# Six places instead of four for the raw sequence blocks of a DFT and MLP kernel's y phases

## The chip, the cores and the metric

The kernel runs on one core of a Trainium2 chip. Its metric is the time of one execution on the device, in microseconds (us). Matmuls run on TensorE, elementwise work on VectorE and ScalarE, a few small operations on GpSimd, and every DMA is issued from SyncE's queue (SP), in the order of the program.

## The reference

A sequence of 2048 rows with 512 features goes through four residual layers, a Fourier mixing layer and an MLP in turn, twice. Everything is float32.

```python
def _A_ref(x, dft_seq_re, dft_seq_im, dft_hid_re, dft_hid_im):
    a = jnp.einsum("bsd,ed->bse", x, dft_hid_re)
    b = jnp.einsum("bsd,ed->bse", x, dft_hid_im)
    return jnp.einsum("ts,bse->bte", dft_seq_re, a) - jnp.einsum("ts,bse->bte", dft_seq_im, b)

def _B_ref(x, w1, w2, w3, w4):
    h = _gelu(_layernorm(x) @ w1)
    hs = (four groups of columns, shifted by +1, -1, +2, -2 rows) @ w2
    x1 = x + hs
    return x1 + _gelu(_layernorm(x1) @ w3) @ w4

x = x + _A_ref(_layernorm(x), ...)
x = x + _B_ref(_layernorm(x), ...)
x = x + _A_ref(_layernorm(x), ...)
x = x + _B_ref(_layernorm(x), ...)
```

## The kernel before, in words

**Stages.** There are two layers, 0 and 1, each a Fourier mixing layer and an MLP. The mixing layer works on four chunks `c` of 512 output columns of the sequence. A chunk has an *x phase* and then a *y phase*, except that chunk 0 of layer 0 has one plain phase. Each phase has eight steps `k`, one for each pair of 128-row tiles of the sequence. The products with the hidden matrices (`hs`) of chunk `c - 1` are woven into the x phase of chunk `c`; after chunk 3 they stand alone, and the MLP (`by_pairs`) follows.

**Products in three matmuls.** Every float32 operand is split into a high part (a cast on ScalarE) and a low part (a subtraction on VectorE), and a product is three matmuls of 128x128 by 128x512: high by high, high by low, low by high (`mm3`, lines 282 to 284). A step of an x or y phase calls `mm_half`, which makes six matmuls. A y step `k` calls it four times, so 24 matmuls.

**Raw blocks and the ring.** The sequence weights (`ws`) come from DRAM in *pieces* of 128x1024 floats, 512 KB, into one of four *places* `raw0` to `raw3`. From a place, the engines make an *item* in one of four *ring* slots: `stage_one` makes the sum and the high part, `stage_two` the low part. A y step takes one pair of pieces and makes two items of it, `by1` and `by0`. Each is a difference of the two pieces (VectorE, L234), its high part (ScalarE, L235) and its low part (VectorE, L245). An x step makes a plain item (cast on ScalarE, L228, low part on VectorE, L245) and an item `one` (L230, L231, L245) of one piece. `stream()` hands the next item to the matmuls, after `prefetch` has made as many later ones as the ring has room for.

**What sets the order.** The code runs in the order in which it is written (a manual schedule), so each engine's list of instructions is fixed when the kernel is built. A semaphore lets an instruction wait for the writer or the last reader of its data. `issue_dma` emits loads of pieces as early as the rule allows: piece `i` goes to place `i % 4`, and its DMA is emitted once the stages that read piece `i - 4` have been emitted. On SP's queue it then waits for these readers, and everything behind it waits as well. Other DMAs stand in the same queue: `X1` loads and stores (`tmp` to and from `x1d`), reloads of tiles `xs` from `x1d` in chunk 3, and the turned tile (`turned0` stored to `zd`, L604, and read back into `zt0f`, L609), which the MLP's first products need.

**Memory.** All these tiles lie in one arena at fixed word addresses. `EXT` is a region of six tiles of 512 words, of which the tile `ay4` takes four during the mixing layer. `STG` is a region of 1024 words that holds staged MLP weights: `w4_raw` is loaded there at hook 2 of some x phases and read at hook 10. The places `raw0` to `raw3` lie at `RAWS` and share their memory with the MLP's scratch tiles `rest0` to `rest7` and `gt`.

Of the kernel before, what the change touches and what calls it, by code (L numbers as in the profile page):

```python
# [8 lines left out]
F32 = mybir.dt.float32  # L9
# [5 lines left out]
S, D, F = 2048, 512, 1376  # L15
# [4 lines left out]
CH = 512  # L20
# [14 lines left out]
RAW = 4  # L35
# [8 lines left out]
def spectral_mlp_kernel(ctx: ExitStack, tc: tile.TileContext, x, ws, hs, w1, w2, w34, out):  # L44
# [35 lines left out]
    EXT = RNG + RING * 4 * CH  # L80
    RAWS = EXT + 6 * D
    STG = RAWS + RAW * 2 * CH + 32
    nc.alloc_sbuf_tensor("arena", [P, STG + 2 * CH], F32)

    def at(name, word, *shape, dtype=F32R):
        return nc.alloc_sbuf_tensor_at(name, [P, *shape], dtype, offset=base + 4 * word).ap()

    def both(name, word, *shape):
        return at(name, word, *shape), at(name + "f", word, *shape, dtype=F32)
# [13 lines left out]
    rg = [[at(f"rg{i}{g}", RR + (4 * i + g) * 2 * CH, 2, CH) for g in range(KD)] for i in range(2)]  # L103
    ring, ringf = zip(*(both(f"ring{i}", RNG + i * 4 * CH, 2, 2, CH) for i in range(RING)))
    raw_at = [at(f"raw{i}", RAWS + i * 2 * CH, 2, CH, dtype=F32) for i in range(RAW)]

    blk, blkf = {}, {}
    for i, word in (("11", H3), ("21", H3 + 4 * CH), ("12", RNG), ("22", RNG + 4 * CH)):
# [15 lines left out]
    def xt(j):  # L124
        return xs[j // 2][:, j % 2]
# [17 lines left out]
        return tmps[(count["tmp"] - 1) % len(tmps)]  # L143


    pieces, items, w_items, w_pieces = [], [], [], []

    def piece(src, a=0, b=2):
        pieces.append((src, a, b))
        return len(pieces) - 1  # L150

    def item(kind, *ids, span=(0, 2), dest=None):
        items.append((kind, ids, span, dest))

    def y_order():
        order = [(k, kind) for k in range(NP) for kind in ("by1", "by0")]
        order[-3], order[-2] = order[-2], order[-3]
        return order

    for layer in range(LAYERS):  # L160
        for c in range(NC):
            if layer == 0 and c == 0:
                for k in range(NP):
                    item("plain", piece(ws[c, k][:, 2:4]))
                    item("plain", piece(ws[c, k][:, 0:2]))
                continue
            for k in range(NP):
                if c:
                    for h in range(NP):
                        if HAT[h] == k:  # L170
                            item("plain", piece(hs[HORDER[h % 4]]))
                p = piece(ws[c, k][:, 2:4])
                item("plain", p)
                item("one", p, span=(0, 1))
            ps = [(piece(ws[c, k][:, 2:4]), piece(ws[c, k][:, 0:2])) for k in range(NP)]
            for k, kind in y_order():
                item(kind, *ps[k])
        for o in HORDER:
            item("plain", piece(hs[o]))
        w_items.append(len(items))  # L180
        for i in range(2):
            item("plain", piece(w1[i]), dest=w12[i])
        for i in range(2):
            item("plain", piece(w2[i]), dest=w12[2 + i])
        w_pieces.append(len(pieces))
    uses = {}
# [1 line left out]
        for i in it[1]:  # L188
            uses.setdefault(i, []).append((n, "two" if it[0] == "plain" else "one"))
    raws, slots, sums = {}, {}, {}  # L190
    state = {"dma": 0, "one": 0, "two": 0, "use": 0, "made": 0, "done": 0, "limit": 0, "load": w_pieces[0]}
    x_left = [(0, 1), (1, 1)] + [(j, 2) for j in range(2, NT, 2)]

    def load_x():
        if x_left:
            j, n = x_left.pop(0)
            rows(xs[j // 2][:, j % 2 : j % 2 + n], x, j, n, True)
# [5 lines left out]
    def issue_dma(upto=None):  # L203
        while state["dma"] < (state["load"] if upto is None else upto):
            i = state["dma"]
            if i >= RAW and any(n >= state[stage] for n, stage in uses[i - RAW]):
                break
            src, a, b = pieces[i]
            raws[i] = raw_at[i % RAW]
            nc.sync.dma_start(raws[i][:, a:b], src)  # L210
            state["dma"] += 1
            if i % 2 and i > 3:
                load_x()
# [154 lines left out]
    def xp_sums(k):  # L368
        ax_sums(k)
        ay_sums(k)  # L370
# [1036 lines left out]
    def w4_split(i):  # L1407
        for n in (i - 5, i - 4, i - 3):
            if 0 <= n <= NF:
                w, wf = w4_in[n % 4]  # L1410
                if n == i - 5:
                    nc.vector.tensor_tensor(w[:, 1], wf[:, 1], w[:, 0].bitcast(F32), op=ALU.subtract)
                    nc.sync.dma_start(w4_from[n][1], w.bitcast(F32))
                elif n == i - 4:
                    nc.scalar.copy(w[:, 0], wf[:, 1])
                else:
                    nc.sync.dma_start(wf[:, 1], w4_from[n][0])
# [26 lines left out]
    for layer in range(LAYERS):  # L1444
# [4 lines left out]
        for c in range(NC):  # L1449
            if layer == 0 and c == 0:  # L1450
                raws[0] = raw_at[0]
                for i in (1, 0):
                    load_x()
                    nc.sync.dma_start(raws[0][:, i], pieces[0][0][:, i])
# [84 lines left out]
            def hook(i):  # L1539
                k, odd = divmod(i, 2)  # L1540
                if layer == 0 and c == 1:
                    if i == 1:
                        xp_sums(NP - 1)
                    if i == 2:
                        xp_highs(NP - 1, False)
                    if i == 3:
                        xp_lows(NP - 1, False)
                    w4_split(2 * NP + i)
                if c == 0:
                    if layer:  # L1550
                        for step, f in zip((0, 0, 1), (ay_sums, ay_highs, ay_lows)):
                            if i == step:
                                f(5)
                            if i == step + 10:
                                f(6)
                        for k, first, stages in (
                            (6, X6, (xp_stats, xp_norm, ax_sums, ax_highs, ax_lows)),
                            (7, X7, (xp_stats, xp_norm, ax_sums, ax_highs, ax_lows)),
                        ):
                            for step, f in zip((0, 1, 3, 4, 6), stages):  # L1560
                                if i == first + step:
                                    f(k)
                    return
                if (layer, c) in W4_AT:
                    w4_sums(W4_AT[layer, c], i)
                j = (c - 1) * TC
                if i == 4:
                    rows(X1, xin, j, 2, True)
                if i == 9:
                    rows(X1, x1d, j, 2, False)  # L1570
                if i == 10:
                    rows(X1, xin, j + 2, 2, True)
                if c == NC - 1 and i in BACK:
                    rows(xs[BACK[i] // 2], x1d, BACK[i], 2, True)
                if c == NC - 1 and i in (12, 15):
                    for j in (0, 1) if i == 12 else (2, 3):
                        normed_act(tmp[:, j], xt(j), ln2[j])
# [16 lines left out]
                    turn_in(ztf[0])  # L1594

            y_phase(c, hook)

        tmps[:] = singles
        count["tmp"] = 0
# [79 lines left out]
```

## Time and profile before

| | |
|---|---|
| runs | 1429.75, 1428.42, 1429.76 us; median 1429.75 |
| the profiled execution's own time | 1429.24 us |
| its span, first to last instruction | 1427.3 us |
| TensorE busy | 1420.0 us, 6261 matmuls |
| VectorE busy | 1168.8 us |
| ScalarE busy | 732.1 us |
| granted TensorE clock | 1.00 |
| DMA | 307.57 MB, mean 215 GB/s |

The span leaves out 1.9 us at the ends of the execution, so a change of the span is a change of the time. In the rows of the profile, a timeline row has the start in us, the duration in us, the engine, the line, the operation and the tiles (out, then in); in brackets stands how long the engine was idle just before and which instruction ended that. A row of the chain has the start, the duration and what the chain went through. PE is TensorE, DVE VectorE, ACT ScalarE, and SPq is SyncE's DMA queue.

### The profile page before, as it was taken

How to read it: one execution, taken by the hardware profiler on the slowest of the kernel's cores; microseconds unless marked ns; L12 is line 12 of the kernel's file. 1: busy time of each engine (PE TensorE's matmuls, PEld its weight loads, DVE VectorE, ACT ScalarE, POOL GpSimd, SP SyncE). 2: the span in 40 equal slices, each digit the busy share in tenths (PEclk: the TensorE clock that was granted, in tenths of full speed). 3: DMA queues.
4: the chain of work that ended last, by engine and by line, in shares of the span. 5: the costliest groups of instructions: out<-in, count | busy, mean ns of one | idle time of the engine just before them, and what ended most of it. 6: DMA issues, size and time to landing. Idle time of an engine off the chain costs nothing.

```text
span 1427.3 us, 17317 instructions
## 1 busy us (share of the span) xinstructions
PE 1420.0 (99%) x6261; PEld 1173.8 (82%) x6261; DVE 1168.8 (82%) x1642; ACT 732.1 (51%) x992; POOL 79.7 (6%) x105
## 2 busy tenths in 40 slices
PE   9999999999999999999999999999999999999998
PEld 7888888888888888888888888888877888888887
DVE  7986998988979888666799989889889787656676
ACT  5663464455565754434455644544555665433351
POOL 2100000000002000000000000000000020000000
PEclk9999999999999999999999999999999999999999
DMA  7866656657754857944645566575777458477764
GB/s 253 278 207 206 206 191 223 212 175 270 270 163 121 290 199 253 362 159 164 223 160 191 182 231 211 175 244 184 232 250 240 139 156 309 159 243 282 241 206 159
DMA packets 127828, 307.57 MB, mean 215 GB/s; under 512 B 9216, under 2 KB 50176, under 8 KB 124544
## 3 DMA queue, kind: packets, MB, share of 16 engines
q1 hardware_dynamic: 127744, 306.48, 64.2%
q8 instruction: 49, 0.80, 0.2%
q14 instruction: 35, 0.29, 0.1%
HBM read 252.18 MB, written 54.26 MB: 215 GB/s over the span
## 4 chain that ended last, share of the span: by engine, by line
PE 96%; DVE 2%; DMA 2%; issue 0%; SPq 0%; ACT 0%; DVEq 0%
PE psd L283 10%; PE psd L282 10%; PE psd L284 10%; PE psa L283 8%; PE psa L282 8%; PE psa L284 8%; PE psc L283 7%; PE psc L284 7%; PE psc L282 7%; PE psb L283 7%; PE psb L282 7%; PE psb L284 7%; DMA raw<-in_ws 2%; DVE ring L245 1%; DVE ring2f L234 0%
## 5 line engine op out<-in xcount | busy, mean ns | idle before, releaser
L228 ACT CAST ring<-raw 128x1024 fp32r<-128x1024 f32 x127 | 132.9, 1052 | 80.3 <-PE psd L284 41.1
L245 DVE TENSOR_TENSOR ring<-raw,ring 128x1024 fp32r<-128x1024 f32 x126 | 153.4, 1219 | 12.8 <-ACT ring L228 12.6
L282 PE MATMUL psd<-ring,rr 128*128 128x512 f32 x208 | 80.9, 389 | 0.0
L283 PE MATMUL psd<-ring,rr 128*128 128x512 f32 x208 | 80.9, 389 | 0.0
L284 PE MATMUL psd<-ring,rr 128*128 128x512 f32 x208 | 80.9, 389 | 0.0
L322 POOL TENSOR_TENSOR rs<-ve,mhalf 128x4 f32<-128x4 f32 x16 | 28.7, 1796 | 609.6 <-DVE nm L321 609.6
L301 POOL TENSOR_TENSOR rs<-ve,mhalf 128x2 f32<-128x2 f32 (+2 forms) x33 | 28.8, 872 | 547.5 <-DVE nb L300 528.6
L235 ACT CAST ring<-ring0f 128x1024 fp32r<-128x1024 f32 x28 | 29.5, 1054 | 57.7 <-DVE ring0f L234 57.7
L619 ACT ACTIVATE tmp<-rest 128x512 f32<-128x512 f32 x30 | 19.0, 632 | 73.2 <-DVE rest L468 72.8
L245 DVE TENSOR_TENSOR ring<-ring1f,ring 128x512 fp32r<-128x512 f32 (+1 forms) x56 | 53.2, 950 | 0.7 <-ACT ring L231 0.7
L330 ACT ACTIVATE tmp<-xs,nb,rs 128x512 f32<-128x512 f32 x56 | 43.2, 808 | 14.4 <-POOL nb L302 13.1
L283 PE MATMUL psb<-ring,ay 128*128 128x512 f32 x128 | 50.2, 392 | 0.4 <-DVE ring L245 0.4
L283 PE MATMUL psc<-ring,ay 128*128 128x512 f32 x128 | 49.9, 390 | 0.3 <-DVE ring L245 0.3
L282 PE MATMUL psb<-ring,ay 128*128 128x512 f32 x128 | 49.8, 389 | 0.0
L284 PE MATMUL psb<-ring,ay 128*128 128x512 f32 x128 | 49.8, 389 | 0.0
L284 PE MATMUL psc<-ring,ay 128*128 128x512 f32 x128 | 49.8, 389 | 0.0
L282 PE MATMUL psc<-ring,ay 128*128 128x512 f32 x128 | 49.8, 389 | 0.0
L235 ACT CAST ring<-ring1f 128x1024 fp32r<-128x1024 f32 x28 | 29.5, 1054 | 39.2 <-DVE ring1f L234 39.2
L282 PE MATMUL psa<-ring,ay 128*128 128x512 f32 x126 | 49.2, 390 | 0.3 <-ACT rr00f L501 0.3
L283 PE MATMUL psa<-ring,ay 128*128 128x512 f32 x126 | 49.1, 389 | 0.0
L282 PE MATMUL psd<-ring,ay 128*128 128x512 f32 x126 | 49.0, 389 | 0.0
L283 PE MATMUL psd<-ring,ay 128*128 128x512 f32 x126 | 49.0, 389 | 0.0
(657 smaller groups left out, 4439.9 us busy)
## 6 DMA issues: line engine op xcount, KB each, us to landing
raw<-in_ws SPq DMA_DIRECT2D x183, 512.0 KB, 5.0
w4r<-w4d SPq DMA_DIRECT2D x66, 512.0 KB, 4.4
raw<-in_hs SPq DMA_DIRECT2D x56, 512.0 KB, 3.6
w3b<-w3d SPq DMA_DIRECT2D x14, 1792.0 KB, 7.9
w3d<-w3b SPq DMA_DIRECT2D x5, 1792.0 KB, 6.9
x1d<-tmp SPq DMA_DIRECT2D x12, 512.0 KB, 6.2
xs<-x1d SPq DMA_DIRECT2D x12, 512.0 KB, 5.2
w4d<-w4in SPq DMA_DIRECT2D x11, 512.0 KB, 5.0
```

Source lines behind the costliest of these rows:

```text
L228: nc.scalar.copy(dest[:, a:b, 0], r[0][:, a:b])
L235: nc.scalar.copy(dest[:, :, 0], lo)
L245: nc.vector.tensor_tensor(lo, src, hi.bitcast(F32), op=ALU.subtract)
L282: nc.tensor.matmul(o, lh, rh, start=first, stop=False, skip_group_check=more)
L283: nc.tensor.matmul(o, lh, rl, start=False, stop=False, skip_group_check=more)
L284: nc.tensor.matmul(o, ll, rh, start=False, stop=last, skip_group_check=more)
L301: nc.gpsimd.tensor_tensor(rs[:, :n], ve[:, :n], mhalf[:, 0, :n], op=ALU.pow)
L322: nc.gpsimd.tensor_tensor(rs, ve, mhalf[:, :, :2], op=ALU.pow)
L330: nc.scalar.activation(o, s, AF.Identity, bias=mr[2], scale=mr[1])
L619: nc.scalar.activation(g_of, ps_of, AF.Gelu_apprx_tanh)
```

## The change

Two more places, `raw4` in the last two tiles of `EXT` and `raw5` in `STG`, may hold raw blocks, but only blocks of y phases (`y_pieces`), and only while `state["wide"]` is set. It is set at hook 11 of the x phase that precedes, so from its second half on, and cleared when the y phase's code has been emitted. The rule of four places in turn is replaced by a choice: of the places whose piece has no reader left to be emitted, the one that has been free longest (lowest piece number). Pieces are still loaded in the same order.

```diff
--- before.py
+++ after.py
@@ -103,6 +103,7 @@
     rg = [[at(f"rg{i}{g}", RR + (4 * i + g) * 2 * CH, 2, CH) for g in range(KD)] for i in range(2)]
     ring, ringf = zip(*(both(f"ring{i}", RNG + i * 4 * CH, 2, 2, CH) for i in range(RING)))
     raw_at = [at(f"raw{i}", RAWS + i * 2 * CH, 2, CH, dtype=F32) for i in range(RAW)]
+    raw_at += [at(f"raw{RAW + i}", word, 2, CH, dtype=F32) for i, word in enumerate((EXT + 4 * D, STG))]
 
     blk, blkf = {}, {}
     for i, word in (("11", H3), ("21", H3 + 4 * CH), ("12", RNG), ("22", RNG + 4 * CH)):
@@ -143,7 +144,7 @@
         return tmps[(count["tmp"] - 1) % len(tmps)]
 
 
-    pieces, items, w_items, w_pieces = [], [], [], []
+    pieces, items, w_items, w_pieces, y_pieces = [], [], [], [], set()
 
     def piece(src, a=0, b=2):
         pieces.append((src, a, b))
@@ -173,6 +174,7 @@
                 item("plain", p)
                 item("one", p, span=(0, 1))
             ps = [(piece(ws[c, k][:, 2:4]), piece(ws[c, k][:, 0:2])) for k in range(NP)]
+            y_pieces.update(i for p in ps for i in p)
             for k, kind in y_order():
                 item(kind, *ps[k])
         for o in HORDER:
@@ -188,7 +190,8 @@
         for i in it[1]:
             uses.setdefault(i, []).append((n, "two" if it[0] == "plain" else "one"))
     raws, slots, sums = {}, {}, {}
-    state = {"dma": 0, "one": 0, "two": 0, "use": 0, "made": 0, "done": 0, "limit": 0, "load": w_pieces[0]}
+    held = {i: None for i in range(len(raw_at))}
+    state = {"wide": False, "dma": 0, "one": 0, "two": 0, "use": 0, "made": 0, "done": 0, "limit": 0, "load": w_pieces[0]}
     x_left = [(0, 1), (1, 1)] + [(j, 2) for j in range(2, NT, 2)]
 
     def load_x():
@@ -203,10 +206,18 @@
     def issue_dma(upto=None):
         while state["dma"] < (state["load"] if upto is None else upto):
             i = state["dma"]
-            if i >= RAW and any(n >= state[stage] for n, stage in uses[i - RAW]):
+            free = [
+                r
+                for r, p in held.items()
+                if (r < RAW or state["wide"] and i in y_pieces)
+                and (p is None or all(n < state[stage] for n, stage in uses[p]))
+            ]
+            if not free:
                 break
             src, a, b = pieces[i]
-            raws[i] = raw_at[i % RAW]
+            r = min(free, key=lambda r: (-1 if held[r] is None else held[r], r))
+            held[r] = i
+            raws[i] = raw_at[r]
             nc.sync.dma_start(raws[i][:, a:b], src)
             state["dma"] += 1
             if i % 2 and i > 3:
@@ -1449,6 +1460,7 @@
         for c in range(NC):
             if layer == 0 and c == 0:
                 raws[0] = raw_at[0]
+                held[0] = 0
                 for i in (1, 0):
                     load_x()
                     nc.sync.dma_start(raws[0][:, i], pieces[0][0][:, i])
@@ -1546,6 +1558,8 @@
                     if i == 3:
                         xp_lows(NP - 1, False)
                     w4_split(2 * NP + i)
+                if i == 11:
+                    state["wide"] = True
                 if c == 0:
                     if layer:
                         for step, f in zip((0, 0, 1), (ay_sums, ay_highs, ay_lows)):
@@ -1594,6 +1608,7 @@
                     turn_in(ztf[0])
 
             y_phase(c, hook)
+            state["wide"] = False
 
         tmps[:] = singles
         count["tmp"] = 0
```

The program has the same instructions on every engine. On TensorE, VectorE, ScalarE and GpSimd their order is the same, and their line numbers are up to 15 higher. On SP's queue the order differs near the y phases, and the places differ. The first place is the beginning of the y phase of chunk 3 in layer 1. In the rows, `raw2_186` is place 2 and `in_ws` the sequence weights. Before:

```order
L1442 DMA w4s4_94<-w4sum_279 128x2048
L201 DMA xs1_150<-x1d_76 128x2x512
L210 DMA raw2_186<-in_ws 128x1024
L210 DMA raw3_187<-in_ws 128x1024
L201 DMA xs2_151<-x1d_76 128x2x512
L210 DMA raw0_184<-in_ws 128x1024
L210 DMA raw1_185<-in_ws 128x1024
L210 DMA raw2_186<-in_ws 128x1024
L210 DMA raw3_187<-in_ws 128x1024
```

Now:

```order
L1453 DMA w4s4_94<-w4sum_281 128x2048
L204 DMA xs1_150<-x1d_76 128x2x512
L221 DMA raw5_189<-in_ws 128x1024
L221 DMA raw4_188<-in_ws 128x1024
L221 DMA raw3_187<-in_ws 128x1024
L221 DMA raw0_184<-in_ws 128x1024
L204 DMA xs2_151<-x1d_76 128x2x512
L221 DMA raw1_185<-in_ws 128x1024
L221 DMA raw2_186<-in_ws 128x1024
```

The pair of blocks behind `xs1` goes to the new places, and the next pair stands ahead of the load of `xs2` with both of its blocks, into places 3 and 0.

The second place is the rest of that y phase on SP's queue, with the store of `X1` (`x1d` from `tmp`), the store of the turned tile, and the first load of a hidden matrix (`in_hs`). Before:

```order
L210 DMA raw0_184<-in_ws 128x1024
L210 DMA raw1_185<-in_ws 128x1024
L201 DMA x1d_76<-tmp_68 128x2x512
L210 DMA raw2_186<-in_ws 128x1024
L210 DMA raw3_187<-in_ws 128x1024
L604 DMA zd1_78<-turned0_157 32x16x128 x4
L210 DMA raw0_184<-in_ws 128x1024
L210 DMA raw1_185<-in_ws 128x1024
L210 DMA raw2_186<-in_ws 128x1024
L210 DMA raw3_187<-in_ws 128x1024
L210 DMA raw0_184<-in_hs 128x1024
```

Now:

```order
L221 DMA raw5_189<-in_ws 128x1024
L221 DMA raw4_188<-in_ws 128x1024
L221 DMA raw3_187<-in_ws 128x1024
L221 DMA raw0_184<-in_ws 128x1024
L204 DMA x1d_76<-tmp_68 128x2x512
L221 DMA raw1_185<-in_ws 128x1024
L221 DMA raw2_186<-in_ws 128x1024
L615 DMA zd1_78<-turned0_157 32x16x128 x4
L221 DMA raw5_189<-in_ws 128x1024
L221 DMA raw4_188<-in_ws 128x1024
L221 DMA raw3_187<-in_hs 128x1024
```

The store of `x1d` and the store of the turned tile both stand two loads further back: four loads of this phase follow the first, where there were six, and two follow the second, where there were four.

The third place is where the first blocks of layer 1 are loaded, on SP's queue among the loads of MLP weights (`w4r`) in the last part of layer 0. Before:

```order
L801 DMA w4r2_219<-w4d1_98 128x1024
L210 DMA raw0_184<-in_ws 128x1024
L801 DMA w4r3_221<-w4d2_99 128x1024
L801 DMA w4r0_215<-w4d3_100 128x1024
L201 DMA x2d_79<-xs4_153 128x2x512
L801 DMA w4r1_217<-w4d4_101 128x1024
L210 DMA raw1_185<-in_ws 128x1024
```

Now:

```order
L812 DMA w4r2_221<-w4d1_98 128x1024
L221 DMA raw2_186<-in_ws 128x1024
L812 DMA w4r3_223<-w4d2_99 128x1024
L812 DMA w4r0_217<-w4d3_100 128x1024
L204 DMA x2d_79<-xs4_153 128x2x512
L812 DMA w4r1_219<-w4d4_101 128x1024
L221 DMA raw3_187<-in_ws 128x1024
```

The order is the same, but the first two blocks go to places 2 and 3 instead of 0 and 1.

## The prediction

> **What bounds the kernel now.** I read the page first (busy shares, chain that ended last), then the list of TensorE's waits, then the timeline around each of them, then the chain in that stretch.
>
> ```profile
> span 1427.3 us, 17317 instructions
> PE 1420.0 (99%) x6261; PEld 1173.8 (82%) x6261; DVE 1168.8 (82%) x1642; ACT 732.1 (51%) x992; POOL 79.7 (6%) x105
> ...
> PE 96%; DVE 2%; DMA 2%; issue 0%; SPq 0%; ACT 0%; DVEq 0%
> ```
>
> TensorE is busy for 1420.0 of 1427.3 us with 6261 matmuls, so 0.227 us each (1420.0 / 6261). The change takes away no matmul. It can only win what TensorE loses between matmuls, and of the 7.3 us without it a part is the start and the end, where the change does nothing. The list of waits names all that lies between:
>
> ```profile
> PE psb L283 <- DVE ring L245: 0.4, 1, 0.4
> PE psc L283 <- DVE ring L245: 0.3, 1, 0.3
> PE psa L282 <- ACT rr00f L501: 0.3, 1, 0.3
> ```
>
> All three are in one place, the y phase of chunk 3 in layer 1. The page models a matmul's end, so the loss is better read from starts. TensorE's timeline there:
>
> ```profile
> 1053.29 0.39 PE L284 MATMUL psb<-ring,ay 128*128 128x512 f32 x1
> 1053.97 0.50 PE L282 MATMUL psa<-ring,ay 128*128 128x512 f32 x1 [0.30 <-ACT rr00f L501]
> 1054.31 0.40 PE L283 MATMUL psa<-ring,ay 128*128 128x512 f32 x1
> ...
> 1058.19 0.39 PE L282 MATMUL psb<-ring,ay 128*128 128x512 f32 x1
> 1059.00 0.50 PE L283 MATMUL psb<-ring,ay 128*128 128x512 f32 x1 [0.42 <-DVE ring L245]
> 1059.33 0.39 PE L284 MATMUL psb<-ring,ay 128*128 128x512 f32 x1
> ...
> 1080.77 0.39 PE L282 MATMUL psb<-ring,ay 128*128 128x512 f32 x1
> 1081.06 0.50 PE L283 MATMUL psb<-ring,ay 128*128 128x512 f32 x1
> 1081.39 0.40 PE L284 MATMUL psb<-ring,ay 128*128 128x512 f32 x1
> ...
> 1083.71 0.39 PE L282 MATMUL psc<-ring,ay 128*128 128x512 f32 x1
> 1084.42 0.50 PE L283 MATMUL psc<-ring,ay 128*128 128x512 f32 x1 [0.33 <-DVE ring L245]
> 1084.76 0.40 PE L284 MATMUL psc<-ring,ay 128*128 128x512 f32 x1
> ```
>
> From the first to the third start of a group there should be 2 x 0.227 = 0.454 us. The groups take 1.02, 1.14, 0.62 and 1.05 us, so they lose 0.57, 0.69, 0.17 and 0.60 us: 2.03 us together, restart included. That is 0.14% of the kernel, and nearly everything that this change can reach.
>
> **Why TensorE waits there.** VectorE makes two steps for each y block (L234 the difference of two raw blocks, L245 its low part), ScalarE one (L235, the high part). Their timelines, VectorE's first, and the load of raw blocks in the chain:
>
> ```profile
> 1047.07 1.22 DVE L245 TENSOR_TENSOR ring<-ring0f,ring 128x1024 fp32r<-128x1024 f32 x1
> 1049.67 1.22 DVE L234 TENSOR_TENSOR ring2f<-raw,raw 128x1024 f32<-128x1024 f32 x1 [1.38 <-PE psa L284]
> ...
> 1057.72 1.22 DVE L245 TENSOR_TENSOR ring<-ring3f,ring 128x1024 fp32r<-128x1024 f32 x1
> ...
> 1072.97 1.23 DVE L234 TENSOR_TENSOR ring2f<-raw,raw 128x1024 f32<-128x1024 f32 x1 [0.91 <-DMA raw<-in_ws]
> ...
> 1082.01 1.22 DVE L234 TENSOR_TENSOR ring1f<-raw,raw 128x1024 f32<-128x1024 f32 x1 [1.00 <-DMA raw<-in_ws]
> 1083.15 1.22 DVE L245 TENSOR_TENSOR ring<-ring0f,ring 128x1024 fp32r<-128x1024 f32 x1
> ```
>
> ```profile
> 1050.98 1.05 ACT L235 CAST ring<-ring2f 128x1024 fp32r<-128x1024 f32 x1 [0.74 <-DVE ring2f L234]
> ...
> 1053.36 1.04 ACT L501 COPY rr00f<-psa 128x512 f32<-128x512 f32 x2
> ```
>
> ```profile
> 1043.93 5.62 DMA raw<-in_ws
> ...
> 1065.03 7.81 DMA raw<-in_ws
> ...
> 1076.86 5.02 DMA raw<-in_ws
> ```
>
> VectorE stands idle for 1.38, 0.91 and 1.00 us before three L234, and each time a load has just landed: 1043.93 + 5.62 = 1049.55 before 1049.67; 1072.84 before 1072.97; 1081.88 before 1082.01. The first idle time is put down to psa's matmul by the timeline, but to the load by the chain. I take the load. The slot ring2 held the last plain block of the x phase, whose last reader is the psb matmul below, done at 1047.85 + 0.39 = 1048.24, and VectorE itself was free at 1047.07 + 1.22 = 1048.29.
>
> ```profile
> 1047.85 0.39 PE L284 MATMUL psb<-ring,ax 128*128 128x512 f32 x1
> ```
>
> From 1049.67 VectorE then works without a pause until L245 at 1057.72 ends at 1058.94 and lets TensorE go on at 1059.00. The psa wait is the same chain through ScalarE: its cast at 1050.98 waits for VectorE, and the copy that empties bank psa (L501) stands behind it.
>
> **The change part by part.** No instruction is added or removed; VectorE, ScalarE, GpSimd and TensorE keep their order. Only loads move. A y load goes into the place freed three pairs earlier instead of two. One pair feeds 24 matmuls, 24 x 0.227 = 5.4 us, so from the second wrap a load can start about 5.4 us sooner.
>
> *First pair into the new places (rows raw5, raw4 behind the load of xs1).* They need no reader to finish in this phase, so they start right behind xs1 instead of at 1037.89 and 1043.93.
>
> ```profile
> 1036.07 0.50 SPq L201 DMA_DIRECT2D xs<-x1d  x1
> 1037.89 0.57 SPq L210 DMA_DIRECT2D raw<-in_ws  x1
> ```
>
> Their landing is set by the queue of transfers before them, of which the list of issues has (one transfer each):
>
> ```profile
> xs<-x1d SPq DMA_DIRECT2D x1, 512.0 KB, 8.4
> ...
> raw<-in_ws SPq DMA_DIRECT2D x1, 512.0 KB, 7.8
> ```
>
> xs1 lands at 1036.07 + 8.4 = 1044.5, the raw block behind it at 1037.89 + 7.8 = 1045.7: 1.2 us for 512 KB in a full queue. Two loads behind xs1 then land at 1045.7 and 1046.9. VectorE could start at 1048.3, so its idle 1.38 us go. Bounds: from 0 (the second load lands where it does now, at 1049.55) to 1.38 us; I take 1.38, since 1046.9 leaves 1.4 us of room.
> With 1.38 us, ring3's L245 ends at 1057.56. TensorE, without its 0.57 us loss, wants that block at 1058.19 + 0.23 - 0.57 = 1057.85. The copy L501, 0.3 us too late now, comes 1.38 us sooner. Both losses go: 0.57 + 0.69 = 1.26 us.
> The Trainium skill, "DMA: Bandwidth & Descriptors", section "Anatomy of one DMA", gives 2.0 us plus bytes / 436e3 for a transfer (fitted on GpSimd's path). That is an estimate of 3.2 us for 512 KB; the three landings above took 5.0 to 7.8, so the trace does not agree where other loads are queued. By the page the load at 1043.93 would land at 1047.1, before VectorE was free, and the 1.38 us would not be the load's: that is the first rival, 1428.5.
>
> *The later pairs.* The loads at 1065.03 and 1076.86 wait for a pair that is now one pair older, so they start about 5.4 us sooner, against idle times of 0.91 and 1.00 us. VectorE gains 1.38 + 0.91 + 1.00 = 3.29 us up to the L245 at 1083.15, TensorE arrives 1.26 + 0.17 us sooner and needs it 0.60 us sooner still: 2.03 in all. Both losses go, 0.77 us. Next in line is the ring of four slots: VectorE then waits for TensorE, which costs nothing.
>
> *What is moved back.* The load of xs2 and the store of x1d now stand behind two more y loads on SP's queue; so does the store of the turned tile (L604), but the pair right ahead of it waits for the readers of the same pair as the one ahead of it did. xs2 is normed only after the y phase, 192 x 0.227 = 43.6 us of matmuls away. X1, which the x1d store reads, is overwritten at k = 7, five or more pairs (27 us) later. Cost nothing; without that cover a delay would be about one pair, 5.4 us.
>
> *The other y phases.* TensorE's list shows no wait in them, so nothing is won there, and loads that come sooner only wait longer for their readers.
>
> *The seam of the layers.* Places rotate, so the first load of layer 1 goes to raw2, where the MLP's scratch tiles rest4 and rest5 lie, no longer to raw0.
>
> ```profile
> 686.71 0.63 ACT L619 ACTIVATE tmp<-rest 128x512 f32<-128x512 f32 x1 [1.68 <-DVE rest L468]
> ...
> 690.44 0.42 SPq L210 DMA_DIRECT2D raw<-in_ws  x1
> ```
>
> Their last reader ends at 687.34, the issue comes at 690.44: 3.1 us of room, so nothing.
>
> Sum against the profiled execution: 1429.24 - 1.26 - 0.77 = 1427.2 us. The median of the runs, 1429.75, is 0.5 us above that execution and the fastest run 0.8 below it. I carry 0.2 of it: 1427.4.
>
> **The rivals.**
> *It is the ring, not the load.* If the 1.38 us are ended by the matmul that the timeline names, the first two losses stay and only 0.77 us go: 1428.5. The same comes out if the extra pair lands after 1049. For: the timeline's row, and three landings over 5 us. Against: the reader of ring2 was done at 1048.24.
> *The loads do not come sooner.* If the queue of transfers is full all through the phase, two places more only lengthen it: 1429.2 to 1429.8. Against: 1.2 us for 512 KB is 430 GB/s, while a pair in 5.4 us needs 194.
> *Slower: the turned tile comes late.* Its store and its load back (zt0f) use the same transfers as the loads that now come earlier.
>
> ```profile
> 1088.65 0.42 SPq L609 DMA_DIRECT2D zt0f<-zd  x1
> ...
> zt0f<-zd SPq DMA_DIRECT2D x1, 1024.0 KB, 9.4
> ...
> 1103.05 1.05 ACT L426 CAST zt<-zt0f 128x1024 fp32r<-128x1024 f32 x1
> ```
>
> It lands at 1098.05 and is read at 1103.05. It decides from 5.0 us of delay, and every microsecond beyond counts; twice the 9.4 us would be 4.4 beyond, in each of the two layers: 1427.2 + 8.8 = 1436. Against: no other load is queued in that stretch that was not there before.
> The Trainium skill, "TensorE: Matmul & The Clock Gate", section "HAM oscillation", adds that gaps over about 3.4 us halve TensorE's clock for a while, an estimate of some 1.7 us more for each; no gap here is that long.
>
> **How the numbers follow.** Forecast (all four losses go) 0.70; ring or late pair 0.14; no sooner 0.09; slower 0.04; something larger that also quiets the rest of the kernel 0.03. The runs shown lie 1.3 us apart, so half of that, 0.7, is added at both ends: low 1427.3 - 0.7 = 1426.6; high 1428.8 (between the first two rivals) + 0.7 = 1429.5. About 0.2% (2.9 us) is what a measurement of this kernel can tell from no change. The forecast stays inside it by 0.5 us, which the scatter can overcome: faster 0.13, same 0.83, slower 0.04.
>
> **What would show it.** In the profile after: no TensorE wait in chunk 3's y phase of layer 1; VectorE's idle time before the L234 rows gone or ended by TensorE; loads there issued more than 10 us before their L234; the chain without raw loads. I am wrong if the 1.38 us remain with the loads landed by 1048, or if a wait shows up behind zt0f, xs2 or the seam.

## The result, and the profile after

| | before | after |
|---|---|---|
| median of 13 runs each, us | 1429.5 (1427.85 to 1431.24) | 1426.69 (1426.21 to 1427.57) |
| ratio, 95% interval | | 0.9982 (0.9974 to 0.9989) |
| the profiled execution's own time, us | 1429.24 | 1426.82 |
| its span, us | 1427.3 | 1424.9 |

The changed kernel is faster by 2.8 us at the median, 0.2%; the profiled executions differ by 2.4 us. The forecast was 1427.4 within 1426.6 to 1429.5, so the time lies inside the range, 0.7 us under the predicted one. The interval leaves out no change (0.1 to 0.3% faster), although the prediction reckoned that 0.2% could hardly be told from it. The runs also scatter less: 1.4 us from the fastest to the slowest where it was 3.4. In the experiments below one of eleven executions of the changed kernel took 3823 us; the median of 1426.65 there counts it, and would be 0.1 us lower without it.

The page of the changed kernel, in the lines that answer to the first ones shown of before:

```profile
span 1424.9 us, 17302 instructions
PE 1418.9 (100%) x6261; PEld 1174.5 (82%) x6261; DVE 1169.3 (82%) x1642; ACT 733.5 (51%) x992; POOL 79.7 (6%) x105
...
PE 96%; DVE 2%; ACT 1%; issue 1%; DMA 0%; POOL 0%; DVEq 0%; SPq 0%; ACTq 0%; POOLq 0%
```

TensorE has the same 6261 matmuls; the 15 instructions fewer in the first line are semaphore instructions. Transfers stood for 2% of the chain that ended last, and now for 0%. The list of waits has two rows for TensorE, and both belong to the start of the program:

```profile
PE psd L138 <- POOL mhalf L56: 1.4, 1, 1.4
PE psb L425 <- DVE rr L338: 1.0, 1, 1.0
```

The three waits of the y phase of chunk 3 in layer 1 are gone. VectorE's timeline in that phase shows why. Lines are 11 higher: the difference of two raw blocks is L245, its low part L256.

```profile
1047.07 1.22 DVE L256 TENSOR_TENSOR ring<-ring0f,ring 128x1024 fp32r<-128x1024 f32 x1
1048.44 1.22 DVE L245 TENSOR_TENSOR ring2f<-raw,raw 128x1024 f32<-128x1024 f32 x1 [0.15 <-DMA raw<-in_ws]
...
1056.50 1.22 DVE L256 TENSOR_TENSOR ring<-ring3f,ring 128x1024 fp32r<-128x1024 f32 x1
...
1070.73 1.21 DVE L245 TENSOR_TENSOR ring2f<-raw,raw 128x1024 f32<-128x1024 f32 x1
...
1078.68 1.21 DVE L245 TENSOR_TENSOR ring1f<-raw,raw 128x1024 f32<-128x1024 f32 x1
```

The idle times of 1.38, 0.91 and 1.00 us before the three L234 of the kernel before have become 0.15, 0 and 0. The low part of ring3 starts at 1056.50 instead of 1057.72. The timeline of TensorE at the worst of the four places, where it lost 0.69 us:

```profile
1057.59 0.39 PE L293 MATMUL psb<-ring,ay 128*128 128x512 f32 x1
1057.82 0.46 PE L294 MATMUL psb<-ring,ay 128*128 128x512 f32 x1
1058.11 0.39 PE L295 MATMUL psb<-ring,ay 128*128 128x512 f32 x1
```

From the first to the third start there are 0.52 us where 0.454 is the undisturbed pace: 0.07 us are lost, and this is all that the phase loses. Read in the same way (starts further apart than 0.227 us, added up over the gaps above 0.25 us), the phase lost 2.03 us before, and the y phase of chunk 3 in layer 0 lost 0.11 before and 0 now.

The rest of the gain shows when the two executions are set side by side, matmul by matmul. The changed kernel is 2.15 us faster over the y phase of chunk 3 in layer 1 and 0.15 over that in layer 0; in every stretch between, the other y phases and the seam of the layers among them, the two are level within 0.1 us. Its first 15 us are 0.13 longer, which differs by some tenths from execution to execution. And behind the last matmul it is 0.17 us faster. The last matmuls, before and after:

```profile
1423.26 0.28 PE L284 MATMUL psc<-hib,u 128*128 128x256 f32 x1
```

```profile
1421.03 0.28 PE L295 MATMUL psc<-hib,u 128*128 128x256 f32 x1
```

From there to the end of the span there are 1427.3 - 1423.26 = 4.04 us before and 1424.9 - 1421.03 = 3.87 after. This comes again: three profiles of the kernel before and three of experiments built on it have 4.0 to 4.1 us there, the changed kernel and six experiments built on it 3.8 to 3.9. Its cause is open. So some 0.2 us of the gain have nothing to do with the y phases, and every experiment that is built on the changed kernel contains them.

The issues and landings, SP's timeline first and then the issues between 1037.2 and 1037.9 us (the columns of the second are number, KB each, median us from issue to landing):

```profile
1036.60 0.72 SPq L221 DMA_DIRECT2D raw<-in_ws  x1
...
1071.32 0.35 SPq L221 DMA_DIRECT2D raw<-in_ws  x1
```

```profile
raw<-in_ws SPq DMA_DIRECT2D x2, 512.0 KB, 10.7
```

The load of `xs1` ahead of them, issued at 1036.13:

```profile
xs<-x1d SPq DMA_DIRECT2D x1, 512.0 KB, 9.6
```

The pair for the new places is issued from 1036.60 on, straight behind the load of `xs1`. The second of its loads is the one that VectorE waits 0.15 us for: it lands just before 1048.44, and not at 1046.9. `xs1` landed at 1036.13 + 9.6 = 1045.7, 9.6 us after its issue where it took 8.4 before; the two blocks landed behind it at 1047.0 and 1048.4 (10.4 and 11.0 us after their issues at 1036.60 and 1037.36), 1.3 and 1.4 us apart. The last load of the phase is issued at 1071.32 instead of 1076.86, so 5.5 us sooner.

### The profile page after: what moved, and what is told of

It is laid out like the page before. It is cut to its first block, busy times and chain, and to the rows that moved or that the text cites. A ratio compares the mean times of both kernels' runs of the same rounds, so it can differ in the third digit from the quotient of the medians.

```text
span 1424.9 us, 17302 instructions
## 1 busy us (share of the span) xinstructions
PE 1418.9 (100%) x6261; PEld 1174.5 (82%) x6261; DVE 1169.3 (82%) x1642; ACT 733.5 (51%) x992; POOL 79.7 (6%) x105
## 4 chain that ended last, share of the span: by engine, by line
PE 96%; DVE 2%; ACT 1%; issue 1%; DMA 0%; POOL 0%; DVEq 0%; SPq 0%; ACTq 0%; POOLq 0%
PE psd L293 9%; PE psd L295 9%; PE psd L294 9%; PE psa L293 8%; PE psa L295 8%; PE psa L294 8%; PE psc L294 7%; PE psc L295 7%; PE psc L293 7%; PE psb L293 7%; PE psb L294 7%; PE psb L295 7%; DVE ring L256 0%; DVE xs L971 0%; DVE ay L406 0%
## 5 line engine op out<-in xcount | busy, mean ns | idle before, releaser
L256 DVE TENSOR_TENSOR ring<-raw,ring 128x1024 fp32r<-128x1024 f32 x126 | 153.4, 1220 | 13.1 <-ACT ring L239 12.9
L256 DVE TENSOR_TENSOR ring<-ring1f,ring 128x512 fp32r<-128x512 f32 (+1 forms) x56 | 53.2, 951 | 0.7 <-ACT ring L242 0.7
L293 PE MATMUL psa<-ring,ay 128*128 128x512 f32 x126 | 49.0, 389 | 0.0
L294 PE MATMUL psa<-ring,ay 128*128 128x512 f32 x126 | 49.0, 389 | 0.0
L295 PE MATMUL psa<-ring,ay 128*128 128x512 f32 x126 | 49.0, 389 | 0.0
```

The costliest lines, as they stand in the source:

```text
L256: nc.vector.tensor_tensor(lo, src, hi.bitcast(F32), op=ALU.subtract)
L293: nc.tensor.matmul(o, lh, rh, start=first, stop=False, skip_group_check=more)
L294: nc.tensor.matmul(o, lh, rl, start=False, stop=False, skip_group_check=more)
L295: nc.tensor.matmul(o, ll, rh, start=False, stop=last, skip_group_check=more)
```

## The experiments

The theory is that the gain is TensorE's waits in chunk 3's y phases, that these waits come from raw blocks landing late for VectorE, and that any place more lets the loads be issued early enough. The rivals are the ring (the slots of the items, and not the loads, hold VectorE back), a gain from other y phases or from the seam of the layers, and SP's order or VectorE's burst of transposes as the real cause. All medians stand beside runs of the kernel before on the same chip. No kernel leaves out or changes a part of the computation; two add loads that nothing reads.

| kernel | median us | before beside it | ratio (95%) |
|---|---|---|---|
| the changed kernel again | 1426.65 | 1428.93 | 0.9984 (0.9975 to 0.9993) |
| new places only in chunk 3, both layers | 1426.74 | 1428.99 | 0.9985 (0.9976 to 0.9993) |
| only in chunk 3 of layer 1 | 1427.54 | 1428.93 | 0.9990 (0.9981 to 0.9999) |
| only in chunk 3 of layer 0 | 1427.91 | 1428.99 | 0.9993 (0.9984 to 1.0002) |
| only for one pair of each y phase | 1427.45 | 1428.93 | 0.9989 (0.9980 to 0.9998) |
| only from step 1 of the y phase on | 1427.40 | 1428.49 | 0.9991 (0.9982 to 1.0000) |
| one new place instead of two | 1426.50 | 1428.93 | 0.9984 (0.9975 to 0.9992) |
| before, transposes spread over four steps | 1429.14 | 1428.49 | 1.0003 (0.9994 to 1.0012) |
| before, 512 KB more per pair | 1436.69 | 1428.49 | 1.0058 (1.0045 to 1.0070) |
| before, 256 KB more per pair | 1432.27 | 1428.99 | 1.0024 (1.0014 to 1.0034) |

**The changed kernel again**, without an edit.

> The changed kernel again, on the chip of the next three. Both theories: about 2.8 us under the kernel before (1426.7 against 1429.5 us).

It gave 1426.65 against 1428.93, a gain of 2.3 us on this chip.

**In which phases the gain lies.** Three kernels set the new places free in some y phases alone:

```diff
 if i == 11:
-    state["wide"] = True
+    state["wide"] = c == NC - 1                  # chunk 3 of both layers
+    state["wide"] = c == NC - 1 and layer == 1   # or: of layer 1 alone
+    state["wide"] = c == NC - 1 and layer == 0   # or: of layer 0 alone
```

> Six places in the y phases of chunk 3 alone, in both layers. Theory, after the run with layer 1 alone (1.4 of 2.3 us): the rest of the gain is chunk 3 of layer 0, which loses time in most executions though hardly in the one shown; so all of the changed kernel's gain, 2.0 to 2.8 us under the kernel before. Rival (the other five y phases give the rest): 1.4 us, as with layer 1 alone.

> The two new places are used in one y phase only, that of chunk 3 in layer 1; all other y phases keep four. Theory (loads of raw blocks land too late where VectorE has no slack, and that is chunk 3 of layer 1): nearly the whole gain, 2.0 to 2.8 us, and no TensorE loss between 1050 and 1085 us. Rival (every y phase gains a little in most executions, the profile shows only the largest): a seventh to a half of the gain, 0.4 to 1.4 us.

> Six places in the y phase of chunk 3 in layer 0 alone. Theory: what layer 1 alone left over, 0.6 to 1.3 us under the kernel before, and no TensorE loss between 345 and 385 us; the losses between 1050 and 1085 us stay. Rival (the other y phases give the rest): under 0.3 us.

Chunk 3 of both layers gains 2.25 us, as much as the changed kernel, so the other y phases and the seam give nothing that these medians can show. Layer 1 alone gains 1.4, not the 2.0 to 2.8 that the theory gave it, and layer 0 alone 1.1; their sum of 2.5 is close to the 2.25, more so as it counts the 0.2 us at the end of the program twice. (The interval of layer 0 alone just takes in no change; that it counts rests on this sum too.) Layer 0 was therefore not worth nothing, though the profile of before shows next to no loss there. The profile of the kernel with the new places in layer 1 alone, which keeps four places in layer 0, shows what was missing. VectorE's timeline and TensorE's in the y phase of layer 0, and the load in the chain:

```profile
344.07 1.23 DVE L245 TENSOR_TENSOR ring2f<-raw,raw 128x1024 f32<-128x1024 f32 x1 [0.71 <-PE psa L295]
```

```profile
352.68 0.39 PE L293 MATMUL psb<-ring,ay 128*128 128x512 f32 x1
353.40 0.50 PE L294 MATMUL psb<-ring,ay 128*128 128x512 f32 x1 [0.33 <-DVE ring L256]
353.74 0.40 PE L295 MATMUL psb<-ring,ay 128*128 128x512 f32 x1
```

```profile
338.99 4.96 DMA raw<-in_ws
```

Here the load lands at 338.99 + 4.96 = 343.95, and the difference starts at 344.07. (The timeline puts the wait down to psa's matmul, the chain to the load.) In the execution of before it started at 343.23:

```profile
343.23 1.23 DVE L234 TENSOR_TENSOR ring2f<-raw,raw 128x1024 f32<-128x1024 f32 x1 [0.20 <-DMA raw<-in_ws]
```

Of the 0.84 us between the two starts, 0.3 are not the load's: by the starts of like matmuls this whole execution is that much later when the phase begins. VectorE waits 0.71 us instead of 0.20. So half a microsecond of a landing decides whether layer 0 loses 0.61 us ((353.74 - 352.68) - 0.454) or 0.11.

**Is one execution of before like the next?** The kernel before, unchanged, for two more profiled executions.

> The kernel before, unchanged, for a second profiled execution. Theory (the loss of both chunk 3 y phases changes from execution to execution, because a load lands some tenths of a us sooner or later): TensorE loses between 0.1 and 1.3 us in chunk 3's y phase of layer 0 and between 0.5 and 2.1 us in that of layer 1, and the two need not repeat 0.11 and 2.05. Rival (the loss is fixed by the order of the loads, and layer 0's 0.11 is what it always costs): 0.1 +- 0.1 and 2.0 +- 0.2 again. Time 1427.5 to 1431 by both.

> The kernel before once more, for a third profiled execution. Theory: again between 0.1 and 1.3 us in layer 0 and between 0.5 and 2.1 us in layer 1, and the spread of the three executions, of both phases together, is over 0.5 us. Rival: 0.1 and 2.0 in each.

They took 1428.17 and 1428.85 us. The first of them, TensorE in layer 0 and in layer 1 at the place that lost 0.69 us:

```profile
352.53 0.39 PE L282 MATMUL psb<-ring,ay 128*128 128x512 f32 x1
353.37 0.50 PE L283 MATMUL psb<-ring,ay 128*128 128x512 f32 x1 [0.45 <-DVE ring L245]
353.70 0.39 PE L284 MATMUL psb<-ring,ay 128*128 128x512 f32 x1
...
1058.57 0.39 PE L282 MATMUL psb<-ring,ay 128*128 128x512 f32 x1
1058.95 0.50 PE L283 MATMUL psb<-ring,ay 128*128 128x512 f32 x1
1059.29 0.39 PE L284 MATMUL psb<-ring,ay 128*128 128x512 f32 x1
```

Here layer 0 loses 0.72 us and layer 1 only 0.27. The losses of the two phases over the three executions of before:

| execution of before | its time | layer 0 | layer 1 |
|---|---|---|---|
| the one that was predicted from | 1429.24 | 0.11 | 2.03 |
| second | 1428.17 | 0.72 | 0.27 |
| third | 1428.85 | 0.21 | 1.30 |

Time less both losses is 1427.1, 1427.2 and 1427.3: what differs between executions of before is these two phases. The theory holds in both phases of the third execution and in layer 0 of the second; layer 1's 0.27 is even less than expected. That the loss is fixed falls. So does the expectation that the losses of layer 1 stay with new places in layer 0 alone: that profile loses only 0.58 us there, with four places. With more places in layer 0 the phase loses 0 in each of four profiles (the changed kernel, chunk 3 of both layers, layer 0 alone, one new place), which fits that the times scatter less.

**Which loads.** One kernel lets only one pair of each y phase use the new places, the other frees the places only from step 1 on, behind the first pair:

```diff
-                if (r < RAW or state["wide"] and i in y_pieces)
+                if (r < RAW or state["wide"] and state["new"] < 2 and i in y_pieces)
...
+            state["new"] += r >= RAW
```

> The new places take one pair of blocks in each y phase, the first one that does not fit into the four, and are left empty after that. Theory: the losses at 1053 and 1058 us go (1.3 us), those at 1081 and 1084 us stay or shrink by what VectorE has gained ahead of them, since the loads of the later pairs again wait for the pair two back: 0 to 0.8 us of loss there, 1.3 to 2.0 us under the kernel before. Rival (the ring's slot ended the first idle time, not the load): the first two losses stay, VectorE still stands about 1.4 us idle before its first late L234, time as before.

```diff
-                if i == 11:
-                    state["wide"] = True
...
             def hook(k):
+                if k == 1:
+                    state["wide"] = True
```

> The new places may be used only from step k = 1 of the y phase on, so they take the sixth pair first and come too late for the pairs behind the losses at 1053 and 1058 us. Theory: these two losses stay (1.3 us), those at 1081 and 1084 us go (0.8 us): 0.6 to 1.0 us under the kernel before. Rival (the later losses only follow from the first ones): all stay, time as before.

They gain 1.5 and 1.1 us, each a part of the whole and near what was expected (1.3 to 2.0 and 0.6 to 1.0). VectorE's timelines in layer 1, of the first and of the second:

```profile
1077.80 1.23 DVE L246 TENSOR_TENSOR ring0f<-raw,raw 128x1024 f32<-128x1024 f32 x1 [1.09 <-DMA raw<-in_ws]
1080.71 1.23 DVE L246 TENSOR_TENSOR ring1f<-raw,raw 128x1024 f32<-128x1024 f32 x1 [0.55 <-DMA raw<-in_ws]
```

```profile
1048.74 1.22 DVE L245 TENSOR_TENSOR ring2f<-raw,raw 128x1024 f32<-128x1024 f32 x1 [0.84 <-DMA raw<-in_ws]
...
1079.25 1.23 DVE L245 TENSOR_TENSOR ring1f<-raw,raw 128x1024 f32<-128x1024 f32 x1 [0.19 <-DMA raw<-in_ws]
```

With the first pair alone the wait before ring2f is gone and the late ones stay (TensorE loses 0.54 us behind them); without the first pair the wait before ring2f stays (TensorE loses 0.71 us in all, where 1.3 were expected to stay) and the late ones shrink. The matmuls and the ring are the same in both. A load that comes sooner removes the wait, so the ring falls as its cause.

**One place instead of two.** The region `STG` is left out:

```diff
-for i, word in enumerate((EXT + 4 * D, STG))]
+for i, word in enumerate((EXT + 4 * D,))]
```

> Five places, raw4 alone. A y block needs both raw blocks of its pair, so one place brings the first block of a pair sooner and the second one as late as before or half a pair sooner. Theory: the idle time of VectorE is set by the second block of the pair; with five places each load waits for a place freed one block earlier than with four, and places are freed in pairs, so in every other pair the second block comes a pair sooner: between no gain and half of it, 0 to 1.4 us. Rival (one more block anywhere is enough, since the late block missed by at most 1.4 us): the whole gain, 2 to 2.8 us.

It has the whole gain, 1426.50 us, as the rival had it; the theory that one place gives at most half was wrong. In its profile VectorE waits once, and TensorE not at all beyond the start:

```profile
1078.83 1.23 DVE L245 TENSOR_TENSOR ring1f<-raw,raw 128x1024 f32<-128x1024 f32 x1 [0.54 <-DMA raw<-in_ws]
```

```profile
PE psd L138 <- POOL mhalf L56: 1.4, 1, 1.4
```

One of the two blocks of the first pair goes to the new place, issued at 1035.91. The other is issued at 1037.47, so neither stands any longer behind the place that came free only at 1043.93 in the kernel before. VectorE's wait of 0.54 us makes TensorE wait nowhere, so VectorE was that far ahead.

The new rule for choosing a place was not run with four places throughout. But where the experiments have four places under it (layer 0 of the kernel with new places in layer 1 alone, and layer 1 of the reverse), SP's queue has the order of before, and the phases lose 0.61 and 0.58 us, no less than some executions of before. Nothing shows it to be a cause by itself.

**Is it the burst on VectorE?** Between the first pair and the loss at 1058 stand four transposes in a row (2.5 us). In the kernel before they are spread over the steps 0 to 3, and the store of the turned tile moves from step 2 to step 4:

```diff
-                if c == NC - 1 and k == 0:
-                    for q in range(TC):
-                        turn_one(turned0, q, tmp[:, q])
-                if c == NC - 1 and k == 2:
+                if c == NC - 1 and k < TC:
+                    turn_one(turned0, k, tmp[:, k])
+                if c == NC - 1 and k == TC:
                     turn_out(turned0)
```

> The kernel before with four places, but the four transposes that VectorE makes at k = 0 of chunk 3's y phase stand at k = 0 to 3, one each, and the store of the turned tile at k = 4. Theory (a late load costs time only because VectorE has these 2.5 us to do behind it): VectorE reaches the L245 that ends at 1058.9 us 1.9 us sooner, so the loss of 0.7 us there goes; the copy of bank psa is ahead of the transposes, so 0.6 us stay at 1053; the later losses stay or move: 0.3 to 0.9 us under the kernel before. Rival (the load alone sets the loss, whatever VectorE does): no change.

It was not faster, 1429.14 against 1428.49, although 0.3 to 0.9 us of gain were expected. TensorE's timeline in layer 1, VectorE's, the load in the chain, and SP's timeline behind it:

```profile
1083.01 0.39 PE L282 MATMUL psc<-ring,ay 128*128 128x512 f32 x1
1084.29 0.50 PE L283 MATMUL psc<-ring,ay 128*128 128x512 f32 x1 [0.89 <-DVE ring L245]
1084.63 0.39 PE L284 MATMUL psc<-ring,ay 128*128 128x512 f32 x1
```

```profile
1081.88 1.23 DVE L234 TENSOR_TENSOR ring1f<-raw,raw 128x1024 f32<-128x1024 f32 x1 [1.84 <-DMA raw<-in_ws]
```

```profile
1075.89 5.86 DMA raw<-in_ws
```

```profile
1076.37 1.17 SPq L604 DMA_DIRECT2D zd<-turned  x2
```

The loss at 1058 is gone, as expected. That at 1053 was to stay and is gone too: VectorE waits only 0.47 us before ring2f in this execution. But then it waits 1.84 us for the last pair, which lands at 1075.89 + 5.86 = 1081.75. TensorE loses 1.16 us there instead of 0.77 (the two last places of before together); layer 0 loses 1.24 at the like place. So spreading the burst does not win time with four places: what it gains at one late load is given back at the next.

How much the burst adds to a late load stays open. The losses at 1053 and 1058 differ between executions anyway (the second execution of before lost 0.27 us there). And the edit also moves the four stores of the turned tile, which are now issued from 1076.37 on, right behind the last pair; that pair took 5.86 us to land where it took 5.02. The two changes were not run apart. In the change that this document is about, VectorE's order is the same, so the burst is not what changed there.

**What a late load costs when the queue is fuller.** The kernel before, with one more load for each pair of the y phase of chunk 3 in layer 1, into the idle region, which nothing reads: the whole piece again, or half of it.

```diff
+            if i in twice:
+                nc.sync.dma_start(idle, src)                  # 512 KB
+                nc.sync.dma_start(idle[:, 0], src[:, 0])      # or: 256 KB
             raws[i] = raw_at[i % RAW]
             nc.sync.dma_start(raws[i][:, a:b], src)
```

> The kernel before with four places, and in the y phase of chunk 3 in layer 1 one more load of 512 KB ahead of every pair, into memory that nothing reads. The queue of transfers took 1.2 us for 512 KB. Theory (the landing of the pair is on the path): each of the three idle times of VectorE grows by about 1.2 us, TensorE loses 1.2 to 3.6 us more there. Rival (the ring's slot or VectorE's own work sets the loss, the transfers have room): under 0.3 us more.

> The kernel before with one more load of 256 KB, half as large as in the last such run, ahead of every pair of chunk 3's y phase in layer 1. Theory (the landing sets the loss, and half of the 7.7 us there came from TensorE's halved clock after a gap of about 3 us): no gap over 2 us, clock 1.00 throughout, TensorE loses 0.6 to 2.5 us more than before in that phase, 1 to 3 us in the time. Rival (the extra issues on SP's queue cost it, whatever their size; or the clock falls at shorter gaps too): 5 us or more, as before with twice the bytes.

They cost 8.2 and 3.3 us, the larger one far more than the 1.2 to 3.6 expected, the smaller one a little more than 1 to 3. With 512 KB, the busy times in the second 20 us of the phase (first of the kernel before, then of this one; the last three numbers are the granted clock, the share of the transfers and GB/s):

```profile
1066.00:1086.00 20.00, 19.67 (x86) 15.59 (x85) 18.05 (x22) 6.74 (x7) 2.24 (x2) 1.00 0.72 226
```

```profile
1066.00:1086.00 20.00, 16.91 (x70) 13.03 (x69) 14.47 (x18) 5.26 (x6) 1.63 (x2) 0.96 0.94 309
```

The transfers' share goes from 0.72 to 0.94, and a block that was issued at 1075.21 took 7.26 us to land. But the extra loads also hold up SP's queue. They all write one region, so four of them wait until the one before has landed, and the pair behind each waits as well. SP's waits (us in total, times, longest), with 512 KB and with 256:

```profile
SPq L213 <- DMA idle<-in_ws: 11.7, 4, 3.7
```

```profile
SPq L213 <- DMA idle<-in_ws: 7.8, 4, 3.1
```

So both runs show that blocks that land later cost time; how much of the delay is the fuller transfers and how much the waiting queue, they do not tell apart. With 512 KB TensorE then waits for 2.80 us, and after that it is slow:

```profile
1081.82 0.39 PE L287 MATMUL psb<-ring,ay 128*128 128x512 f32 x1
1085.01 0.79 PE L288 MATMUL psb<-ring,ay 128*128 128x512 f32 x1 [2.80 <-DVE ring L250]
1085.60 0.63 PE L289 MATMUL psb<-ring,ay 128*128 128x512 f32 x1
1086.03 0.63 PE L287 MATMUL psb<-ring,ay 128*128 128x512 f32 x1
```

```profile
1085.00:1091.00 6.00, 5.99 (x14) 4.70 (x15) 3.48 (x4) 1.05 (x1) 0.00 (x0) 0.50 0.05 20
```

Starts are 0.43 us apart instead of 0.227 for 5.5 us, and the granted clock of this stretch is 0.50. Thirteen matmuls lose 0.20 us each, 2.6 us: about a third of the 7.7 us that this phase loses is the slower pace behind the wait, not the half that the expectation of the second run reckoned with.

## Why the prediction was right, and what it mis-sized

The mechanism was as forecast: all four losses of the y phase of layer 1 went (0.07 us of 2.03 remain), and nothing took their place. By its steps:

- *First pair into the new places.* The load, not the ring, ended the 1.38 us; the two experiments with a part of the pairs show it. The landing was off. It was to be 1046.9 with 1.4 us of room, and was about 1048.4, 0.1 us after VectorE was free: the room was not there, and 0.15 us of the 1.38 stayed. Of the step's two terms the 1.2 us from block to block held (1.3 and 1.4); the landing of `xs1`, taken over from before, was 1.2 us too early. The two losses still went to within 0.07, since ring3's low part came 1.22 us sooner and TensorE needed hardly more.
- *The later pairs.* The 5.4 us by which the loads were to start sooner were 5.5 (1071.32 for 1076.86). Both losses went. The sign that was to show it, issues more than 10 us ahead of their difference, is met by the first pair (1036.60 for 1048.44); for the last load 7.4 us (1071.32 for 1078.68) were enough.
- *What is moved back* and *the seam of the layers* cost nothing: no wait of TensorE stands behind either in the list.
- *What bounds the kernel* set the start and the end of the program at nothing. Behind the last matmul 0.2 us went, for a cause that is open.
- *The other y phases* is the step that was mis-sized. It set them at nothing, because TensorE's list of before shows no wait there. For the phases of chunks 0 to 2 that holds. New places in the y phase of chunk 3 in layer 0 won 1.1 us at the median, the 0.2 us at the end included: the profile on which the sum was made is one execution, and in that one its load landed early (VectorE waited 0.20 us for it, 0.71 and 0.80 in two others).
- *The sum.* Layer 1 was set at 2.03 us from the same single execution, and it was a bad one for this phase: the two others lost 0.27 and 1.30, and the new places in layer 1 alone won 1.4 at the median. Too much for layer 1 and nothing for layer 0 came near the whole by two errors of opposite sign: 2.0 forecast, 2.3 to 2.8 measured. That the sum came this near is luck; that the waits would go was not.

Of the rivals, the ring and "the loads do not come sooner" fall with the first step and the experiments with a part of the pairs. The transfers had room: their share in the first half of the phase, 1046 to 1066, rose from 0.63 to 0.79, and in the second, 1066 to 1086, from 0.72 to 0.75. The late turned tile did not come about either. Its load back is issued 5.5 us sooner, not later, because the loads into raw places ahead of it on the queue are gone sooner too, and it lands within 7.1 us:

```profile
1083.11 0.38 SPq L620 DMA_DIRECT2D zt0f<-zd  x1
```

```profile
zt0f<-zd SPq DMA_DIRECT2D x1, 1024.0 KB, 7.1
```

What stays open: why VectorE waits for the same load not at all in one execution and up to 0.8 us in another. The sizes by layer are rough, too. The three executions of before lose 0.35 us in layer 0 and 1.2 in layer 1 in the mean. Three more profiles have a layer 0 as before (those with new places in layer 1 alone and with extra loads: 0.61, 0.80 and 1.24), one has a layer 1 with four places (0.58). With them the means are 0.6 and 1.0 us, and with the 0.2 at the end 1.9. That is below the 2.3 to 2.8 of the medians, though within their intervals.

## What to carry to other kernels

A wait that hangs on a load that lands just in time is not a fixed number: read it from several executions, and look in the like phases, where the profiled one happens to show none, for how little room their loads have. A single buffer more can be worth as much as two, as it was here, if what the queue waits for is one reader. A fix for one late load in a chain of them can be given back at the next one, as in the run with the spread transposes, so look for what makes all of them early. And an added load is a clean probe only if nothing on its queue has to wait for it.

## What the runs showed of the hardware that was not expected

TensorE's clock fell after shorter idle times than the prediction reckoned with. With 512 KB more per pair, one idle time of 2.80 us was followed by a granted clock of 0.50 over 6 us. With 256 KB more, one of 1.98 us was enough, with another of 1.03 us some 4 us before (in the profiled execution, the slowest of its eight: 1435.01 us where the median is 1432.27):

```profile
1086.21 0.39 PE L287 MATMUL psc<-ring,ay 128*128 128x512 f32 x1
1088.57 0.67 PE L288 MATMUL psc<-ring,ay 128*128 128x512 f32 x1 [1.98 <-DVE ring L250]
1089.04 0.63 PE L289 MATMUL psc<-ring,ay 128*128 128x512 f32 x1
1089.47 0.63 PE L287 MATMUL psc<-ring,ay 128*128 128x512 f32 x1
```

The pace of 0.43 us then lasted for eight starts, 3.5 us, in which the granted clock was 0.53. The Trainium skill, "TensorE: Matmul & The Clock Gate", section "HAM oscillation", puts the limit at idle gaps over about 3.4 us; these two traces, with 2.80 and 1.98 us, do not agree with it as a limit for a single gap. In the kernel before and in the changed one, where no wait within the phases is above 0.5 us, the clock stays at 1.00. Whether one gap of 2 us is enough, or idle times near to each other add up, these runs do not tell apart.

A short wait has a price of its own: after each idle time of 0.3 to 0.9 us in TensorE's rows shown here the next matmul takes 0.50 instead of 0.39 us, and the start behind it comes 0.33 or 0.34 instead of 0.227 us later, 0.11 us each time.
